# Pooled attention and a gated convolution FFN on one core: the division in two steps on VectorE or ScalarE, the score scale in the keys, the order written out anew

## The chip, the cores and the metric

The kernel runs on one core of one Trainium2 chip. The metric is the device time of one execution in microseconds (us), the median of several runs. Engines are named as in the profile: PE is TensorE's matmul stream and PEld its weight loads, DVE is VectorE, ACT is ScalarE, POOL is GpSimd, SP is SyncE. A "q" behind an engine's name means its queue of DMA issues. L697 is line 697 of the kernel before.

## The reference

The inputs are `q`, `k`, `v` of shape (8, 8, 576, 64) (batch, heads, sequence, head size), and the weights `w_in` (512 x 1024), `conv_w` (3 x 1024) and `w_out` (1024 x 512). The output is (8, 576, 512) in float32.

```python
# attention over keys and values that are averaged in runs of 8
k_p = k.reshape(B, H, 72, 8, D).mean(axis=3)
v_p = v.reshape(B, H, 72, 8, D).mean(axis=3)
scores = matmul(q, k_p.transpose(0, 1, 3, 2)) / sqrt(D)
attn = exp(scores - max(scores, axis=-1))
x = matmul(attn / sum(attn, axis=-1), v_p)        # heads side by side: (8, 576, 512)

# gated FFN with a convolution of three taps over the sequence
h = maximum(x @ w_in, 0)
conv_out[s] = sum over k of conv_w[k] * h[s + k - 1]
out = (h * sigmoid(conv_out)) @ w_out
```

## The kernel before

The eight sequences (`b` = 0 to 7) are worked in four groups of two (`g` = 0 to 3). A group's 1152 rows of queries are cut into tiles of 128 rows (`t` = 0 to 8; group 0 has ten, since it splits the tile that both sequences share). Attention is done tile by tile, the FFN sequence by sequence, so that the attention of a later sequence runs beside the FFN of an earlier one.

A tile of attention takes these steps, each a function:

- `att_scores` (PE): the scores of eight heads against 72 pooled keys each, into two PSUM banks.
- `att_max` (VectorE, L608): the negated maximum of each head.
- `att_shift`: it is added to the scores, on VectorE (L620) for 27 tiles and as a matmul on PE (L628) for group 0.
- `att_exp` (ScalarE, L646): the exponent, with the scale 1/64 (an eighth for the mean over 8 keys, which the pooling leaves as a sum, and an eighth for the head size).
- `att_turn` and `att_copy`, or a transposing DMA (`att_send`, L666, groups 2 and 3): the transposed weights.
- `att_values` (PE, L682): the products with the values; a 65th column of each head holds the sum of the weights.
- `att_divide` (VectorE): a reciprocal of the eight sums (L695), and at once the product with it (L697), which gives the tile `x`.
- `att_turn_out` and `att_copy_out`, or a transposing DMA (`att_out`, L706): `x` transposed, as the FFN's input.

Keys are prepared by a pooling matrix `pm` on PE for sequences 0 and 1, and for the others by three additions on VectorE (`pool_pair`, L439) and a matmul with a selection of the identity (`turn_pair` with `pick`, `turn_keys`). Values are prepared by three additions (`prep_v`, L486) and a product with a mask (L490), all on VectorE. Queries are transposed on PE (`prep_q`), in halves or in quarters of the array, and copied (`copy_q`, L534) by VectorE or ScalarE; those of sequences 6 and 7 by a transposing DMA (`q_send`).

The FFN of a sequence: `ffn_in` (PE, L727) and `ffn_relu` (ScalarE, L736) for eight blocks of 128 features; the convolution either on PE (`ffn_conv`, L889), with `ffn_tanh` (L914) and `ffn_gate` (L925, L927), or by taps, for six half sequences (`TAPS`): the middle tap on ScalarE (L862), the two others on VectorE (`ffn_tap`, L864), then `ffn_tap_tanh` (L869) and `ffn_tap_gate`. The gate's product with `h` is L935 (`ffn_times`) behind PE's convolution and L876 behind the taps; "product" below is one of these 16 instructions. Then `ffn_out` (PE, L943), `ffn_copy` (L954) on either engine, and `ffn_store` (L966).

The order of all this is written out by hand. `add` makes a graph of operations, each with the engines that it may run on and a planner's price in us. `order` reads three tables: `ORDER` names each operation in turn (twice its number, plus 1 for the second of its engines, -1 for a fill, a matmul without use that keeps PE busy), `FORMS` says which form of the array a step takes, `PLACES` which buffer or bank. So the program of each engine's queue is fixed, and each engine works through its own in order; across engines it waits by semaphores only where data or buffers need it. All loads go through POOL's queue but the first three, the transposing DMAs and most stores through SP's.

Buffers come in rings: `"v": 3`, `"qp": 4` (queries as loaded), `"x": 4`. The output tiles of group 3 (`late`) lie in halves of the `qp` buffers.

Of the kernel before, what the change touches and what calls it, by code (L numbers as in the profile page):

```python
# [33 lines left out]
class Graph:  # L34
# [32 lines left out]
    SHIFT_PE = ((0, 0), (0, 1), (0, 2), (0, 3), (0, 4), (0, 5), (0, 6), (0, 7), (0, 8), (0, 9))  # L67
    TURN_DMA = 2
    BANKS = 8
    ORDER = (  # L70
# [52 lines left out]
    )  # L123
    FORMS = (
        1, 0, 1, 0, 1, 1, 1, 0, 0, 0, 0, 1, 1, 0, 0, 1, 1, 0, 0, 0, 0, 1, 1, 0, 0, 0, 0, 1, 0, 0, 0, 1, 1, 1, 1, 0, 1, 1, 1, 1,
    )
    PLACES = (
# [50 lines left out]
def kernel(  # L178
# [23 lines left out]
    KW = 2 * Sp  # L202
    SLOTS = 24
    NJ = 5
    KP = NJ * P

    groups = [[0, 1], [2, 3], [4, 5], [6, 7]]
    where = {b: (g, i) for g, bs in enumerate(groups) for i, b in enumerate(bs)}
# [1210 lines left out]
```

## Time and profile before

| | |
|---|---|
| median of 3 runs | 217.14 us (216.84 to 217.48) |
| span of the profiled execution | 216.5 us |
| between that span and the median of the runs | 0.6 us |
| busy: PE, DVE, ACT | 201.9, 193.2, 162.7 us |
| matmuls and their weight loads | 2753 each |
| instructions on DVE, ACT | 334, 278 |
| mean granted clock of TensorE | 0.992 |

The span runs from the first to the last instruction of the profiled execution; a run's time has a little more around it, taken here as the 0.6 us to the median. The busy time of an engine is the time in which at least one of its instructions runs, so that two which overlap at their ends count once. A row of groups names line, engine, operation, output and inputs, count, then busy us and the mean ns of one, then the idle time in front of them and what ended it. A row of the timeline has start and length in us.

### The profile page before, as it was taken

To read this page: it belongs to the slowest core of one execution; us is meant where nothing else is said; L and a number is where in the kernel's file an instruction comes from. 1 tells how busy PE (TensorE), PEld (TensorE's weight loads), DVE (VectorE), ACT (ScalarE), POOL (GpSimd) and SP (SyncE) were. 2 spreads that over 40 slices of the span, in tenths; PEclk is the share of its full clock that TensorE was granted. 3 is DMA by queue.
4 is the path that set the end of the run, shared out by engine and by line. 5 is a ranking of instruction groups with operands and counts; after the bars stand their busy time and mean duration, and the time that the engine had idled before them with its cause. 6 is when DMAs were issued, how large, how long until landed. Compare 5 with 4: busy or idle time off the path is not lost.

```text
span 216.5 us, 6617 instructions
## 1 busy us (share of the span) xinstructions
PE 201.9 (93%) x2753; PEld 137.0 (63%) x2753; DVE 193.2 (89%) x334; ACT 162.7 (75%) x278; POOL 41.5 (19%) x78
## 2 busy tenths in 40 slices
PE   7599999969999999999999899989999999999992
PEld 3557778855788776766776675665656666654451
DVE  7598989999999999999999799999899999998621
ACT  2548885896998887787497594878979999997420
POOL 8644330050052101000000030002201210370000
PEclk9799999999999999999999999999999999999999
DMA  6999999999999999969687634576347745602685
GB/s 210 227 207 209 206 207 208 210 205 206 207 205 206 154 153 179 158 164 165 131 111 100 136 74 89 58 156 148 78 104 153 158 100 123 145 0 51 169 242 171
DMA packets 48833, 33.46 MB, mean 155 GB/s; under 512 B 28300, under 2 KB 43812, under 8 KB 48804
## 3 DMA queue, kind: packets, MB, share of 16 engines
q0 software_dynamic: 15216, 15.40, 43.5%
q1 hardware_dynamic: 32512, 16.13, 36.6%
q10 hardware_dynamic: 1076, 1.52, 2.5%
q8 instruction: 21, 0.34, 0.7%
q14 instruction: 8, 0.07, 0.1%
HBM read 32.52 MB, written 9.44 MB: 194 GB/s over the span
## 4 chain that ended last, share of the span: by engine, by line
PE 45%; DVE 34%; issue 6%; ACT 6%; DMA 5%; SPq 2%; DVEq 0%
PE psum L943 20%; PE psum L727 16%; DVE negm L608 7%; DVE x L697 6%; DVE sd L620 4%; DVE gT L935 4%; DMA hT<-in_k_dram 3%; DVE v L486 3%; DVE gT L927 3%; PE psum L889 2%; DMA out_dram<-osb 2%; DVE r L695 2%; PE psum L682 2%; ACT e L646 2%; DVE gT L925 1%
## 5 line engine op out<-in xcount | busy, mean ns | idle before, releaser
L727 PE MATMUL psum<-xT,w_in_sb 128*128 128x288 bf16 x512 | 74.1, 286 | 2.2 <-DMA xT<-x 1.1
L943 PE MATMUL psum<-w_out_sb,gT 128*128 128x512 bf16 (+1 forms) x296 | 69.5, 374 | 0.7 <-DVE gT L935 0.6
L727 PEld LDWEIGHTS <-w_in_sb 128*128 128x128 bf16 x512 | 47.9, 98 | 19.1 <-issue 2.0
L736 ACT ACTIVATE hT<-psum 128x576 bf16<-128x576 f32 x64 | 40.3, 650 | 14.0 <-PE psum L727 13.4
L943 PEld LDWEIGHTS <-gT 128*128 128x128 bf16 x296 | 27.3, 98 | 26.5 <-issue 0.9
L864 DVE SCALAR_TENSOR_TENSOR tg<-hT,convw,tg 128x576 f32<-128x576 bf16 x48 | 37.6, 815 | 0.5
L608 DVE TENSOR_REDUCE negm<-psum 128x8 f32<-128x576 f32 (+2 forms) x37 | 27.5, 752 | 2.3 <-PE psum L582 1.6
L697 DVE TENSOR_TENSOR x<-psum,r 128x512 bf16<-128x512 f32 (+1 forms) x37 | 25.6, 691 | 1.4
L811 POOL COPY hT<-hT 128x126 bf16<-128x126 bf16 x16 | 7.5, 467 | 97.6 <-ACT hT L736 80.1
L620 DVE TENSOR_TENSOR sd<-psum,negm 128x576 f32<-128x576 f32 x27 | 20.2, 753 | 0.5
L682 PE MATMUL psum<-vm,eT 128*128 128x130 bf16 (+5 forms) x240 | 18.9, 222 | 1.1 <-DVE x L697 0.7
L646 ACT ACTIVATE e<-sd 128x576 bf16<-128x576 f32 x27 | 18.2, 685 | 1.3 <-DVE sd L620 1.1
L954 ACT COPY osb<-psum 128x512 f32<-128x512 f32 x27 | 15.7, 585 | 4.4 <-PE psum L943 4.2
L889 PE MATMUL psum<-hT,dw 64*64 64x288 bf16 (+2 forms) x608 | 18.7, 261 | 0.1
L682 PEld LDWEIGHTS <-eT 128*128 128x128 bf16 (+1 forms) x240 | 15.3, 100 | 5.4 <-DMA eT<-e 1.2
L862 ACT ACTIVATE tg<-hT,convw 128x576 f32<-128x576 bf16 x24 | 18.1, 772 | 0.1
L889 PEld LDWEIGHTS <-dw 64*64 64x64 bf16 x608 | 14.8, 107 | 4.6 <-issue 3.7
L869 ACT ACTIVATE gT<-tg 128x576 bf16<-128x576 f32 x24 | 16.3, 683 | 0.7 <-DVE tg L864 0.5
L914 ACT ACTIVATE gT<-psum 128x576 bf16<-128x576 f32 x20 | 12.9, 651 | 3.9 <-PE psum L889 2.7
L914 ACT ACTIVATE tg<-psum 128x576 bf16<-128x576 f32 x20 | 13.0, 652 | 2.6 <-PE psum L889 1.4
L935 DVE TENSOR_TENSOR gT<-gT,hT 128x2304 bf16<-128x2304 bf16 x10 | 13.5, 1352 | 0.1
L486 DVE TENSOR_TENSOR v<-v 128x1280 bf16<-128x1280 bf16 (+2 forms) x24 | 13.0, 540 | 0.2
(84 smaller groups left out, 234.2 us busy)
## 6 DMA issues: line engine op xcount, KB each, us to landing
out_dram<-osb SPq DMA_DIRECT2D x54, 128.0 KB, 2.4
v<-in_v_dram POOLq DMA_DIRECT2D x8, 512.0 KB, 13.1
qp<-in_q_dram POOLq DMA_DIRECT2D x7, 576.0 KB, 14.4
kk<-in_k_dram POOLq DMA_DIRECT2D x3, 1152.0 KB, 14.6
out_dram<-qp ACTq DMA_DIRECT2D x10, 128.0 KB, 2.7
hT<-in_k_dram SPq DMA_DIRECT2D x2, 576.0 KB, 5.0
w_in_sb<-in_moe_w_in_dram POOLq DMA_DIRECT2D x2, 512.0 KB, 14.2
w_out_sb<-in_moe_w_out_dram POOLq DMA_DIRECT2D x1, 1024.0 KB, 24.7
```

The lines of the kernel that those rows point to most:

```text
L608: nc.vector.tensor_reduce(out=a["m"][0:rows], in_=a["s"][0:rows, :, 0:2 * KW].rearrange("p a (h s) -> p a h s", s=Sp), axis=AX.X, op=OP.ma ...
L620: nc.vector.tensor_tensor(out=a["d"][0:rows], in0=a["s"][0:rows, :, 0:2 * KW].rearrange("p a (h s) -> p a h s", s=Sp), in1=a["m"][0:rows]. ...
L646: nc.scalar.activation(out=dst, in_=src, func=ACT.Exp, scale=1.0 / (POOL * 8.0),)
L682: nc.tensor.matmul(out=a["o"][lo:hi, h // 4, (h % 4) * (D + 1):(h % 4 + x1 - x0) * (D + 1)], lhsT=a["eT"][:, j, lo:hi], rhs=buf("vm", b)[: ...
L697: nc.vector.tensor_tensor(out=a["x"][0:rows].rearrange("p (a h d) -> p a h d", a=2, d=D), in0=ov[:, :, :, 0:D], in1=r[0:rows].unsqueeze(3) ...
L727: nc.tensor.matmul(out=banks(ps)[:, j, 0:SC], lhsT=w_in_block(dc, fb), rhs=buf("xT", g)[:, dc, i * S + j * SC:i * S + (j + 1) * SC], start ...
L736: nc.scalar.activation(out=h_of(b)[:, fb].rearrange("p (a s) -> p a s", a=2), in_=banks(ps)[:, :, 0:SC], func=ACT.Relu, scale=0.5,)
L864: nc.vector.scalar_tensor_tensor(out=acc, in0=h, scalar=w, in1=acc, op0=OP.mult, op1=OP.add)
L889: nc.tensor.matmul(out=banks(pss[r ^ c])[c * D:(c + 1) * D, j, lo:hi], lhsT=dw[r * D:(r + 1) * D, tap * n_fb + fb, :], rhs=hT[r * D:(r + 1 ...
L914: nc.scalar.activation(out=t.rearrange("p (a s) -> p a s", a=2), in_=banks(ps)[:, :, 0:SC], func=ACT.Tanh, scale=0.5,)
L935: nc.vector.tensor_tensor(out=gate, in0=gate, in1=h_of(b)[:, four], op=OP.mult)
L943: nc.tensor.matmul(out=bank(ps)[0:rows, columns], lhsT=buf("gT", g)[:, fb, t * P:t * P + rows], rhs=w_out_sb[:, fb, columns], start=(fb == 0),
```

## The change

- The division becomes two steps of the graph: `att_invert` (the reciprocal, VectorE) and `att_divide` (the product, VectorE or ScalarE), which `ORDER` may place apart. On ScalarE the product is eight activations, one for each head, with the head's reciprocal as a column of scales.
- The product behind the taps' gate, so far the second instruction of `ffn_tap_gate`, becomes a step of its own, `ffn_times`.
- The scale 1/64 leaves the exponent. It stands in the pooling matrix, and in `ident_k`, an identity times 1/64 from which `pick` and `turn_keys` take their columns.
- `att_exp` can work head by head with the negated maximum as bias; the list of tiles that do so, `EIGHT`, is empty.
- The late output tiles stand behind the query copies and transposes of sequences 4 to 7, where it was those of sequence 7.
- `ORDER`, `FORMS` and `PLACES` are new as a whole: other engines for some copies, other forms for some score and query steps (six score tiles and one query in quarters that were in larger parts), 28 fills where there were 17, another order of the loads and of everything else.

```diff
+    EIGHT = ()
     ORDER = (
...
+    KSCALE = 1.0 / (POOL * 8.0)
+    ident_k = const.tile([P, P], BF16, name="ident_k")
...
     def clear_pool_matrix():
-        nc.vector.memset(pm[0:TB, :, 0:Sp], 1.0)
+        nc.vector.memset(pm[0:TB, :, 0:Sp], KSCALE)
...
     def build_pick():
+        nc.vector.tensor_scalar(out=ident_k, in0=ident, scalar1=KSCALE, scalar2=None, op0=OP.mult)
...
             func=ACT.Exp,
-            scale=1.0 / (POOL * 8.0),
...
-    def att_divide(g, t):
+    def att_heads(g, t):
+        return att[g, t]["o"][0:rows_of(g, t), :, 0:4 * (D + 1)].rearrange("p a (h d) -> p a h d", d=D + 1)
+
+    def att_invert(g, t):
+        nc.vector.reciprocal(out=buf("r", g, t)[0:rows_of(g, t)], in_=att_heads(g, t)[:, :, :, D])
+
+    def att_divide(g, t, engine):
         a, rows = att[g, t], rows_of(g, t)
-        r = buf("r", g, t)
-        nc.vector.reciprocal(out=r[0:rows], in_=ov[:, :, :, D])
+        ov, r = att_heads(g, t), buf("r", g, t)
         a["x"] = buf("x", g, t)
+        if engine == "ACT":
+            for n in range(H):
+                nc.scalar.activation(
+                    out=a["x"][0:rows, n * D:(n + 1) * D],
+                    in_=ov[:, n // 4, n % 4, 0:D],
+                    func=ACT.Identity,
+                    scale=r[0:rows, n // 4, n % 4:n % 4 + 1],
+                )
+            return
         nc.vector.tensor_tensor(
...
     def ffn_tap_gate(b, f4):
         nc.vector.tensor_scalar(out=gate, in0=gate, scalar1=1.0, scalar2=None, op0=OP.add)
-        nc.vector.tensor_tensor(out=gate, in0=gate, in1=h_of(b)[:, four], op=OP.mult)
...
-        o = add(dve(0.2, 0.69), key, lambda: att_divide(g, t), after=[o], uses=[x, rr, big])
+        o = add({"DVE": 0.115}, key, lambda: att_invert(g, t), after=[o], uses=[rr, big])
+        o = add({"DVE": 0.61, "ACT": 0.82}, key, None, after=[o], uses=[x, rr, big])
+        o.emit = lambda o=o: att_divide(g, t, o.engine)
...
-            gated = add(dve(0.78, 1.39), w, lambda f4=f4: ffn_tap_gate(b, f4), after=tanh, uses=[htok[b], gtok[g]])
+            o = add(dve(0.78), w, lambda f4=f4: ffn_tap_gate(b, f4), after=tanh, uses=[gtok[g]])
+            gated = add(dve(1.39), w, lambda f4=f4: ffn_times(b, f4), after=[o], uses=[htok[b], gtok[g]])
...
-            osb, free = (token("late", g, t), qdone[7, 0]) if g == 3 else (token("osb", g, t), [])
+            osb, free = (token("late", g, t), [x for n in range(4, B) for x in qdone[n, 0]]) if g == 3 else (token("osb", g, t), [])
```

More of the change, by code (lines that the diff above doesn't have):

```diff
@@ L70 @@
     ORDER = (
[52 rows of a table removed]
[55 rows of a table added]
     )
     FORMS = (
-        1, 0, 1, 0, 1, 1, 1, 0, 0, 0, 0, 1, 1, 0, 0, 1, 1, 0, 0, 0, 0, 1, 1, 0, 0, 0, 0, 1, 0, 0, 0, 1, 1, 1, 1, 0, 1, 1, 1, 1,
+        1, 1, 0, 0, 1, 1, 1, 1, 1, 1, 1, 1, 1, 1, 1, 0, 1, 1, 1, 1, 1, 0, 1, 0, 0, 0, 0, 1, 1, 0, 0, 1, 1, 1, 1, 1, 1, 1, 1, 1,
     )
     PLACES = (
[17 rows of a table removed]
[18 rows of a table added]
     )
@@ L260, with by_head @@
     add = graph.add
+    def by_head(g, t):
+        return (g, t) in Graph.EIGHT
     def shift_by_dve(g, t):
@@ L375, in build_pick @@
                     out=pick[:, hh].rearrange("p (s f a e) -> p s f a e", s=2, f=2, a=2)[:, :, f],
-                    in_=ident.rearrange("p (s a hh f e) -> p s a hh f e", s=2, a=2, hh=2, f=2)[:, :, :, hh, f],
+                    in_=ident_k.rearrange("p (s a hh f e) -> p s a hh f e", s=2, a=2, hh=2, f=2)[:, :, :, hh, f],
                 )
@@ L470, in turn_keys @@
                     lhsT=buf("kk", g)[:, c, 0:D],
-                    rhs=ident[:, i * D:(i + 1) * D],
+                    rhs=ident_k[:, i * D:(i + 1) * D],
                     start=True,
@@ L640, in att_exp @@
         e = a["e"] = buf("e", g, t)
+        if by_head(g, t):
+            for n in range(H):
+                r, k = n // 4, n % 4
+                at = (k // 2 * 4 + r * 2 + k % 2 if a["by_rows"] else n) * Sp
+                nc.scalar.activation(
+                    out=e[0:rows, at:at + Sp],
+                    in_=a["s"][0:rows, r, k * Sp:(k + 1) * Sp],
+                    func=ACT.Exp,
+                    bias=a["m"][0:rows, r, k:k + 1],
+                )
+            return
         src = a["d"][0:rows].rearrange("p a h s -> p a (h s)") if shift_by_dve(g, t) else a["s"][0:rows, :, 0:2 * KW]
@@ L689, in att_values @@
                 )
-    def att_divide(g, t):
+    def att_heads(g, t):
[3 more added lines that the diff above has]
+    def att_divide(g, t, engine):
         a, rows = att[g, t], rows_of(g, t)
-        ov = a["o"][0:rows, :, 0:4 * (D + 1)].rearrange("p a (h d) -> p a h d", d=D + 1)
-        r = buf("r", g, t)
-        nc.vector.reciprocal(out=r[0:rows], in_=ov[:, :, :, D])
+        ov, r = att_heads(g, t), buf("r", g, t)
         a["x"] = buf("x", g, t)
+        if engine == "ACT":
+            for n in range(H):
+                nc.scalar.activation(
+                    out=a["x"][0:rows, n * D:(n + 1) * D],
+                    in_=ov[:, n // 4, n % 4, 0:D],
+                    func=ACT.Identity,
+                    scale=r[0:rows, n // 4, n % 4:n % 4 + 1],
+                )
+            return
         nc.vector.tensor_tensor(
@@ L872, in ffn_tap_gate @@
         g, i = where[b]
-        four = slice(4 * f4, 4 * f4 + 4)
-        gate = buf("gT", g)[:, four, i * S:(i + 1) * S]
+        gate = buf("gT", g)[:, 4 * f4:4 * f4 + 4, i * S:(i + 1) * S]
         nc.vector.tensor_scalar(out=gate, in0=gate, scalar1=1.0, scalar2=None, op0=OP.add)
-        nc.vector.tensor_tensor(out=gate, in0=gate, in1=h_of(b)[:, four], op=OP.mult)
     def ffn_conv(b, f2, pss):
@@ L1113, in add_pair @@
             t = token("ps", n=2)
-            o = add({"PE": 0.26}, key, lambda b=b, t=t: turn_keys(b, t), after=[prev, c0], uses=[t, kk[g]], mode=HALF, count=36)
+            o = add({"PE": 0.26}, key, lambda b=b, t=t: turn_keys(b, t), after=[prev, picked], uses=[t, kk[g]], mode=HALF, count=36)
             c = add(either(0.76, 0.71), key, None, after=[o], uses=[t, ktok[b]])
@@ L1209, in add_att @@
         o = add(dve(0.75), key, lambda: att_max(g, t), after=[o], uses=[ng, s])
-        if shift_by_dve(g, t):
+        if by_head(g, t):
+            o = add({"ACT": 0.9}, key, lambda: att_exp(g, t), after=[o], uses=[e, s, ng, lim])
+        elif shift_by_dve(g, t):
             sd = token("sd", g, t)
@@ L1326, in add_ffn @@
             if f2 % 2 and cross:
-                gated = add(dve(0.78, 1.39), w + 6 * f2 + Graph.GATE, lambda f4=f4: ffn_tap_gate(b, f4), after=tanh[f4], uses=[htok[b], gtok[g]])
+                o = add(dve(0.78), w + 6 * f2 + Graph.GATE, lambda f4=f4: ffn_tap_gate(b, f4), after=tanh[f4], uses=[gtok[g]])
+                gated = add(dve(1.39), w + 6 * f2 + Graph.GATE, lambda f4=f4: ffn_times(b, f4), after=[o], uses=[htok[b], gtok[g]])
                 gdone.setdefault(b, []).append(gated)
```

142 rows, old and new, of tables (ORDER, PLACES) are left out of this document.

## The prediction

> **What bounds the kernel now.** I read the page first: busy shares, the 40 slices, the chain that ended last.
>
> ```profile
> span 216.5 us, 6617 instructions
> PE 201.9 (93%) x2753; PEld 137.0 (63%) x2753; DVE 193.2 (89%) x334; ACT 162.7 (75%) x278; POOL 41.5 (19%) x78
> DVE  7598989999999999999999799999899999998621
> ACT  2548885896998887787497594878979999997420
> PEclk9799999999999999999999999999999999999999
> PE 45%; DVE 34%; issue 6%; ACT 6%; DMA 5%; SPq 2%; DVEq 0%
> ```
>
> VectorE (DVE) is nearly full from the third slice to the 36th, but the chain belongs to TensorE (PE) for more of the span. Where one hands over to the other stands in the chain in order of time, its last part (start, length, what), and the stretches say how full each engine is (columns: stretch, width, then busy time of PE, PEld, DVE, ACT and POOL, clock, DMA).
>
> ```profile
> 142.52 0.61 DVE x L697
> ...
> 144.72 0.51 PE psum L682 x6
> ...
> 199.10 13.16 PE psum L943 x68
> ...
> 212.28 0.42 DVE qp L954
> ```
>
> ```profile
> 100.00:120.00 20.00, 18.68 (x343) 13.66 (x340) 19.56 (x36) 13.51 (x23) 0.00 (x0) 1.00 0.86 131
> 120.00:140.00 20.00, 19.91 (x256) 13.14 (x257) 18.34 (x30) 14.96 (x26) 3.21 (x8) 1.00 0.48 85
> 140.00:160.00 20.00, 18.91 (x215) 11.64 (x208) 19.15 (x31) 16.68 (x30) 3.37 (x8) 1.00 0.58 124
> 160.00:180.00 20.00, 20.00 (x142) 12.78 (x141) 19.76 (x30) 18.45 (x32) 3.09 (x8) 1.00 0.60 130
> 180.00:190.00 10.00, 10.00 (x67) 6.36 (x65) 9.72 (x13) 9.88 (x18) 2.35 (x4) 1.00 0.57 133
> ```
>
> Until 144.7 VectorE sets the pace: attention and preparation pass through it, and PE waits for their tiles. From 144.72 to 212.28 the chain is PE work back to back, while VectorE stays 96 to 99% busy. So time is won by less VectorE work ahead of the hand-over (PE then starts its full stretch earlier) and about as much less behind it (or VectorE becomes the late one). ScalarE (ACT) has 25 to 32% of room from 100 to 140 and almost none from 160 to 190: 28.3 of 30 us.
>
> **VectorE: the division.** The timeline of VectorE around one division (start, length):
>
> ```profile
> 123.05 0.76 DVE L620 TENSOR_TENSOR sd<-psum,negm 128x576 f32<-128x576 f32 x1
> 123.72 0.20 DVE L695 RECIPROCAL r<-psum 128x8 f32<-128x8 f32 x1
> 123.95 0.69 DVE L697 TENSOR_TENSOR x<-psum,r 128x512 bf16<-128x512 f32 x1
> 124.56 0.45 DVE L925 TENSOR_SCALAR gT<-gT 128x1152 bf16<-128x1152 bf16 x1
> ```
>
> The reciprocal starts 0.09 us before the shift in front of it ends; the multiplication, which needs the reciprocal, waits 0.03 past its end. A division costs 124.56 - 123.72 = 0.84 us, of which the reciprocal holds 0.23. Behind it something that doesn't need it could start after 0.20 - 0.09 = 0.11, so standing apart saves 0.12. Written out, the new order keeps 31 multiplications on VectorE; in only 11 of them another VectorE operation stands between reciprocal and multiplication. Six go to ScalarE: tiles (2,2), (2,0), (2,6), (3,2), (3,1), (3,6), as (group, tile). Before: 37 x 0.84 = 31.1 us. After: 20 x 0.84 + 11 x 0.72 + 6 x 0.11 = 25.4. That is **-5.7**. Other neighbours where one needs the one before change in number from 29 to 28 (shift behind its own maximum 13 to 10, tap behind a tap of its block 7 to 13, product behind its own gate 9 to 5): -0.1.
>
> [...]
>
> **VectorE: copies that change engine.** Groups (busy, mean ns of one):
>
> ```profile
> L458 ACT CAST kT<-psum 64x288 bf16<-64x288 f32 x8 | 3.1, 394 | 0.1
> L534 DVE COPY qT<-psum 128x1152 bf16<-128x1152 bf16 x5 | 3.8, 758 | 1.3 <-PE psum L520 1.3
> L534 DVE COPY qT<-psum 128x512 bf16<-128x512 bf16 x1 | 0.4, 425 | 0.1
> L671 DVE COPY eT<-psum 128x640 bf16<-128x640 bf16 x3 | 1.5, 484 | 0.4 <-ACT kT L431 0.4
> L722 DVE COPY xT<-psum 128x512 bf16<-128x512 bf16 x4 | 1.6, 415 | 0.0
> L954 DVE COPY qp<-psum 128x512 f32<-128x512 f32 x3 | 2.1, 689 | 6.0 <-PE psum L943 6.0
> L294 DVE CAST kk<-hT 128x1152 bf16<-128x1152 f32 x1 | 0.7, 742 | 0.0
> ```
>
> Each less 0.09 of overlap. To VectorE: two pair copies (2 x 0.30 by ScalarE's row, VectorE has none), one 512-wide q copy (0.34), two x copies (0.33 and, half as wide, 0.2), one q cast (0.35, as the q copy), one output copy (0.60), the scaled identity (0.1, estimated from these). From it: one 1152-wide q copy (0.67), one e copy (0.39), the k cast (0.65). Net **+0.8**. Two more output copies move to VectorE, but behind the last product of its program, where it idles for PE: nothing.
>
> Sum up to VectorE's last product: -5.7 - 0.1 + 0.8 = **-5.0**.
>
> **The hand-over.** Take PE's value products of tile (3,4), whose division is the piece at 142.52. In both orders exactly the same PE steps stand in front of them, fills left out (17 before, 28 after, placed where PE would wait). VectorE's work in front of them: 29 divisions, after the change 16 whole, 9 apart, 4 with ScalarE: -4.0; one maximum fewer -0.7; four shifts fewer behind their own maximum -0.5; a tap behind a tap +0.1; copies +0.2. That is -4.9: nearly all of the saving lies ahead of the hand-over, and PE's work behind it is the same. The tail is the same too: VectorE's last product (next fence) ends at 203.16, and PE's products for the last sequence's five output tiles follow it, then a copy and a store; after the change the last product is one with taps instead of one with PE's convolution, with the same five tiles behind it.
>
> ```profile
> 201.80 1.36 DVE L935 TENSOR_TENSOR gT<-gT,hT 128x2304 bf16<-128x2304 bf16 x1
> ```
>
> **ScalarE: eight pieces for one.** No row shows a 64-wide activation; these bound it (timeline, then groups):
>
> ```profile
> 151.30 1.44 ACT L862 ACTIVATE tg<-hT,convw 128x576 f32<-128x576 bf16 x2
> 152.63 0.58 ACT L954 COPY osb<-psum 128x512 f32<-128x512 f32 x1
> 153.62 1.74 ACT L736 ACTIVATE hT<-psum 128x576 bf16<-128x576 f32 x3 [0.40 <-PE psum L727]
> ```
>
> ```profile
> L954 ACT COPY osb<-psum 128x512 f32<-128x512 f32 x27 | 15.7, 585 | 4.4 <-PE psum L943 4.2
> L722 ACT COPY xT<-psum 128x256 bf16<-128x256 bf16 x2 | 0.7, 371 | 0.0
> ```
>
> 585 - 371 over 256 columns is 0.836 ns a column. L862, the only activation with a scale column as the divide has, takes 1.33 / 2 = 0.665 us in a row, less 576 columns 0.184 fixed; 64 columns add 0.053: 0.24 us, eight are **1.9 us**. From below, without a price for the scale column (L736, three in 1.74): 0.58 less 0.48 leaves 0.10 fixed, a piece is 0.15 and eight are 1.2. I take 1.9, since its row has the same operand; the planner's price in the diff is 0.82. Six make 11.4 us more on ScalarE, less what leaves with the copies above (the same list, the other way, and two output copies more). The first four, group 2's three and (3,2), stand ahead of the hand-over, where the stretches from 100 to 140 leave ScalarE 11.5 us idle for their 7.6: hidden. The other two stand behind it, (3,1) and (3,6). The first has 3.3 us of room in its stretch of 20, which covers it; the second falls where 28.3 of 30 are taken, and I put its 1.9 us at 94% on the path: **+1.8**. What queues behind a divide on ScalarE is the next relu, tanh or exponent, and behind those PE's banks.
>
> **Edits at nothing.** The 1/64 goes into the pooling matrix and the identity as a power of two, no instruction but the scaled identity; the exponent's scale was part of its instruction. The per-head exponent has an empty list. The gate split is two instructions as before. The late buffers' wait is for q copies and transposes of sequences 4 to 7, long done at the first store of group 3. Transposes of one q in quarters instead of halves and six score tiles in quarters leave PE's time within a few tenths. SP's queue has the q transpose of sequence 6 in front of the first two e transposes instead of behind them; its load comes long before either is due. At the start PE's fills begin behind three more clears; half clock covers the second slice, where this group runs:
>
> ```profile
> 9.37 1.29 PE L406 MATMUL psum<-gT,kk 128*64 128x144 bf16 x18
> ```
>
> Warm, it and its like behind it would be 0.65 shorter each, colder as much longer: 1.3 either way, taken as 0.
>
> **Sum.** Span 216.5 - 5.0 + 1.8 = 213.3. The median of the runs, 217.14, is 0.6 above the span; so **213.9 us**, its own range 212.2 to 215.5.
>
> **Rivals.** *All of it arrives* (ScalarE's room takes all six): 217.1 - 5.0 = 212.1, with a warm start 210.9. For it: PE and VectorE both gain the same 5 us; against it: ScalarE's slices 31 to 36, all at 9.
>
> *ScalarE takes VectorE's place, slower.* Each divide holds ScalarE's queue 1.9 us, and relu, tanh and exponent queued behind it wait; PE waits for their banks. Priced at what exceeds the 0.82 it was placed by, 6 x 1.1 = 6.6: 217.1 - 5.0 + 6.6 = 218.7. It is slower as soon as more than 0.83 us of each divide gets to the path. [...] In the trace 0.184 of a 0.24 piece is fixed. Against this rival: four of six lie in 25 to 32% of room.
>
> *A load comes late.* v of sequence 4 was issued early, into a buffer long free:
>
> ```profile
> 45.59 0.76 POOL L305 DMA_DIRECT2D v<-in_v_dram  x1
> DMA to landing us min/median/max: 18.2/18.2/18.2
> 58.44 0.65 DVE L490 TENSOR_TENSOR vm<-v,mask_wide 128x960 bf16<-128x960 bf16 x1
> 71.87 0.82 DVE L486 TENSOR_TENSOR v<-v 128x1280 bf16<-128x1280 bf16 x1
> ```
>
> It landed at 63.8 and was used at 71.87. In the new order it stands behind two q loads and in the buffer of sequence 2, whose last reader (58.44) ends at 59.1, some 1.7 sooner after the change: issue at 57.4 at best, use due 2.1 sooner, at 69.8. With the 18.2 us of its row it lands at 75.6 and VectorE stands 5.8 us: 219.7. With a queue emptier than at 45, as I expect, it is in time. Half of that is no change: 216.8.
>
> **Chances.** Forecast 0.40; all arrives 0.20; no net change (half of the load's delay, or orders' small waits) 0.10; ScalarE slower 0.22; load late 0.08. Within 0.3% (0.65 us), about what a measurement can tell, is 216.5 to 217.8. Faster: 0.40 + 0.20 + 0.03 of the middle case = 0.63; same 0.07; slower 0.30. The range goes from 210.9 (all, warm) to 218.7 (ScalarE's price), with about a tenth left out on each side.
>
> **What would show it.** Right: VectorE's last product ends near 200; PE's unbroken stretch starts near 140; a reciprocal with a stranger behind it is followed after 0.11; eight pieces take 1.9 us; ScalarE is busy about 10 us longer. Wrong: ScalarE's divide as releaser of waits for relu, tanh or PE's banks above 2 us in sum; an idle VectorE ahead of the v additions of sequence 4; last product not before 203.

## The result, and the profile after

The changed kernel takes 223.64 us (median of 4 runs, 223.22 to 224.42), the kernel before 217.31 us beside it (216.84 to 218.12): ratio 1.030, 95% interval 1.026 to 1.034, slower. The prediction had 213.9 us, in a range of 210.9 to 218.7. Some executions of a kernel take over 1.5% longer than its fastest (three of 12 in the last experiment, up to 227.33 us where the fastest has 216.31); the times and ratios below leave them out.

The page of the changed kernel (span, busy, VectorE in 40 slices, one DMA queue, the chain's shares):

```profile
span 222.1 us, 6965 instructions
...
PE 199.3 (90%) x2890; PEld 135.8 (61%) x2908; DVE 191.1 (86%) x335; ACT 170.8 (77%) x320; POOL 40.7 (18%) x78
...
DVE  7788767969799989899979999999979999999640
...
q8 instruction: 22, 0.36, 0.7%
...
PE 48%; DVE 17%; DMA 11%; ACT 9%; issue 8%; SPq 3%; POOL 2%; DVEq 0%; ACTq 0%; POOLq 0%
```

VectorE is busy 2.1 us less than before, as wanted, and yet the span is 5.6 us longer: of VectorE's slices 5 to 11 only two still have a nine, where before six had one. PE has 137 matmuls and 155 weight loads more. Stretch by stretch, after and then before (stretch, width, busy PE, PEld, DVE, ACT, POOL):

```profile
20.00:60.00 40.00, 33.64 (x758) 24.61 (x758) 31.43 (x55) 28.73 (x49) 8.66 (x15) 1.00 1.23 204
```

```profile
20.00:60.00 40.00, 37.30 (x676) 28.66 (x674) 38.07 (x68) 32.17 (x56) 8.14 (x12) 1.00 1.23 207
```

Between 20 and 60 us all three engines are less busy than before, VectorE by 6.6 us and PE by 3.7, at full clock and with the same load on the DMA. Something stops PE, and the others run dry behind it. The chain of the changed kernel in order of time names it (start, length, what), and shows a divide on ScalarE and the end of the span as well:

```profile
28.80 1.42 issue
...
43.98 1.54 issue
...
56.53 1.58 issue
...
177.53 1.74 ACT x L724 x8
...
211.91 3.54 DMA out_dram<-osb
215.86 0.60 ACT qp L986
216.50 1.05 PE psum L975 x8
217.64 0.42 DVE qp L986
```

"issue" is time in which an engine waits for nothing that the profile shows. PE's timeline around the three places:

```profile
28.42 0.38 PE L531 MATMUL psum<-ident,qp 64*64 64x64 bf16 x24
30.22 0.29 PE L531 MATMUL psum<-ident,qp 64*64 64x64 bf16 x12 [1.42 <-issue]
...
43.13 0.86 PE L921 MATMUL psum<-hT,dw 64*64 64x288 bf16 x26
45.52 0.32 PE L921 MATMUL psum<-hT,dw 64*64 64x63 bf16 x6 [1.53 <-issue]
...
56.15 0.38 PE L975 MATMUL psum<-w_out_sb,gT 128*128 128x512 bf16 x1 [0.16 <-issue]
58.10 1.45 PE L975 MATMUL psum<-w_out_sb,gT 128*128 128x512 bf16 x6 [1.58 <-issue]
```

Each of these stalls falls inside one step, of which all inputs were there: 24 of 36 transposes run, then nothing for 1.4 us, then the other 12. The reading that the experiments below put to the test is that PE's program comes too late. Queue q8, of the kind "instruction", moves 22 packets, 0.36 MB in all, 16 KB each. Number PE's matmuls, weight loads and the 12 entries of its sequencer in order of start: the three stalls stand at 961, 1473 and 1983, which is 193 + 256 n, two off in the last, and one packet arrives for each such 256. (The 193 is read off the stalls.) Worked out from the trace (times in us; "crossed" is when PE starts the instruction at the boundary in front of the block, "stall" the longest pause within a few numbers of its end):

```
after:  block crossed  packet starts  packet ends  PE passes block's end  whole block  stall
 449-705      19.03        +2.97         22.93           24.30               5.27       1.18
 705-961      24.30        +3.71         28.98           30.22               5.92       1.61
 961-1217     30.22        +3.73         34.92           39.83               9.61        -
1217-1473     39.83        +3.35         44.15           45.52               5.69       1.73
1473-1729     45.52        +3.60         50.02           51.44               5.92       0.46
1729-1985     51.44        +4.31         56.65           58.32               6.88       1.95
before, the only one with a stall ahead of 65 us:
1217-1473     39.42        +3.46         43.85           45.15               5.73       0.51
```

Two of the five stalls of the changed kernel have another explanation as well. At 24.30 and at 51.24 the first matmul behind the pause also waits for a copy on ScalarE, and the profile puts the waits down to that:

```profile
PE psum L593 <- ACT xT L756: 1.1, 1, 1.1
...
PE psum L593 <- ACT kT L469: 0.4, 1, 0.4
```

The other three, 5.3 us in all, have none but the program.

In these rows the packet that by this reading holds the next block starts 3.0 to 4.3 us after PE has crossed into the block before it, takes 0.9 to 1.0, and PE goes on 1.2 to 1.7 us behind its end. Where PE stood, a block of 256 instructions took 5.3 to 6.9 us; the one that the changed kernel entered at 92.54 us, with its packet 1.0 us later, took 4.5 and had no stall. The lag is long while the queue of the loads (q0) fills the DMA (the changed kernel's slices 2 to 11, up to 61 us, all at nine tenths or more, with 187 to 212 GB/s): over both kernels 2.0 to 4.3 us in the 15 blocks crossed up to 60 us, 1.7 to 2.5 in the five later ones beside loads, 0.1 to 0.6 where next to nothing else moves, and anything from 0.2 to 2.6 beside the transfers of queue q1; where PE's instructions are long the packet comes up to 1.5 us ahead of the crossing. Behind 65 us no block is late: PE passes its end 1.8 us or more after the packet.

No packet of the two kernels starts more than one block and 1.5 us ahead of PE, and the stalls of 1.6, 1.7 and 2.0 us in the table are the ones that the profile puts down to nothing else.

The balance, up to VectorE's last product (which ends at 207.62, before at 203.16): VectorE's instructions take 3.7 us less, its idle times of over 0.12 us take 8.2 more, 6.8 of them between 20 and 60 us. Behind the last product 14.5 us follow where it was 13.4. That is +4.5 and +1.1, the 5.6 us of the span.

### The profile page after: what moved, and what is told of

It reads as the page before. It is cut to its first block, busy times and chain, and to the rows that moved or that the text cites. A ratio compares the mean times of both kernels' runs of the same rounds, so it can differ in the third digit from the quotient of the medians.

```text
span 222.1 us, 6965 instructions
## 1 busy us (share of the span) xinstructions
PE 199.3 (90%) x2890; PEld 135.8 (61%) x2908; DVE 191.1 (86%) x335; ACT 170.8 (77%) x320; POOL 40.7 (18%) x78
## 4 chain that ended last, share of the span: by engine, by line
PE 48%; DVE 17%; DMA 11%; ACT 9%; issue 8%; SPq 3%; POOL 2%; DVEq 0%; ACTq 0%; POOLq 0%
PE psum L761 17%; PE psum L975 10%; DVE tg L898 9%; DMA kk<-in_k_dram 5%; PE psum L921 5%; PE psum L703 5%; DMA out_dram<-osb 4%; ACT hT L770 2%; DVE gT L967 2%; SPq L998 2%; PE psum L678 2%; PE psum L531 2%; DMA eT<-e 2%; PE psum L593 2%; PE psum L748 2%
## 5 line engine op out<-in xcount | busy, mean ns | idle before, releaser
L761 PE MATMUL psum<-xT,w_in_sb 128*128 128x288 bf16 x512 | 71.4, 286 | 2.5 <-ACT osb L986 1.0
L975 PE MATMUL psum<-w_out_sb,gT 128*128 128x512 bf16 (+1 forms) x278 | 65.8, 373 | 4.0 <-issue 2.2
L770 ACT ACTIVATE hT<-psum 128x576 bf16<-128x576 f32 x64 | 41.2, 661 | 7.2 <-PE psum L761 6.6
L898 DVE SCALAR_TENSOR_TENSOR tg<-hT,convw,tg 128x576 f32<-128x576 bf16 x48 | 38.2, 817 | 1.2 <-ACT tg L896 0.3
L967 DVE TENSOR_TENSOR gT<-gT,hT 128x2304 bf16<-128x2304 bf16 x16 | 21.7, 1369 | 0.2
L731 DVE TENSOR_TENSOR x<-psum,r 128x512 bf16<-128x512 f32 (+1 forms) x31 | 21.1, 683 | 0.7
L921 PEld LDWEIGHTS <-dw 64*64 64x64 bf16 x608 | 15.3, 107 | 5.3 <-issue 4.0
L986 ACT COPY osb<-psum 128x512 f32<-128x512 f32 x25 | 14.7, 591 | 4.3 <-PE psum L975 2.4
```

The costliest lines, as they stand in the source:

```text
L731: nc.vector.tensor_tensor(out=a["x"][0:rows].rearrange("p (a h d) -> p a h d", a=2, d=D), in0=ov[:, :, :, 0:D], in1=r[0:rows].unsqueeze(3) ...
L761: nc.tensor.matmul(out=banks(ps)[:, j, 0:SC], lhsT=w_in_block(dc, fb), rhs=buf("xT", g)[:, dc, i * S + j * SC:i * S + (j + 1) * SC], start ...
L770: nc.scalar.activation(out=h_of(b)[:, fb].rearrange("p (a s) -> p a s", a=2), in_=banks(ps)[:, :, 0:SC], func=ACT.Relu, scale=0.5,)
L898: nc.vector.scalar_tensor_tensor(out=acc, in0=h, scalar=w, in1=acc, op0=OP.mult, op1=OP.add)
L921: nc.tensor.matmul(out=banks(pss[r ^ c])[c * D:(c + 1) * D, j, lo:hi], lhsT=dw[r * D:(r + 1) * D, tap * n_fb + fb, :], rhs=hT[r * D:(r + 1 ...
L967: nc.vector.tensor_tensor(out=gate, in0=gate, in1=h_of(b)[:, four], op=OP.mult)
```

## The experiments

Three theories stood against each other: F, PE's program is fetched too late; D, the divides hold up ScalarE; T, the tail, where ScalarE's copy stands for a store out of a buffer that is used twice. In `ORDER`, an entry of a step is twice its number, plus 1 for its second engine.

**The forms of before in the changed kernel.**

```diff
 FORMS, by step (1: quarters)
-    scores (0,3) (0,6) (0,7) (0,8) (1,3) (1,7) (2,1) (2,3) (2,7): 1
+    ...: 0
-    query steps 1 (both halves), 3 (one), 4 (one): 1
+    ...: 0
-    scores (0,1) (1,1) (1,2): 0
+    ...: 1
```

> The changed kernel with the forms of the kernel before for each score and query step: 16 steps change, 13 of them from quarters back to halves or whole, about 216 PE instructions fewer up to 60 us (5798 in all become about 5510). Theory F (PE's instructions are fetched in blocks of 256, and while the loads saturate the DMA queues a block cannot be run in less than 5.3 to 6.9 us, so PE stands at block ends): the stalls at 24.3, 30.2, 45.5 and 58.1 us go or shrink by two thirds, VectorE's idle from 20 to 60 us falls from 7.9 to about 3, and the time from 223.6 to 219.5 (218.5 to 221). Theory D (ScalarE's divides) and theory T (tail and other waits of the order): no change, 223.6 within 0.7.

Measured 216.94 us where before has 217.87: ratio 0.996 (0.993 to 1.000). Against the changed kernel that is 0.034 of 217 us, 7.3 us (give or take 1.1): the whole loss, and a time below the expected 218.5 to 221. PE's waits for "issue" between 15 and 62 us, of the changed kernel (all, times, longest):

```profile
PEld L531 <- issue: 2.2, 4, 1.5
...
PEld L921 <- issue: 2.1, 2, 1.7
PEld L593 <- issue: 2.1, 5, 1.1
...
PEld L975 <- issue: 1.9, 1, 1.9
```

and with the forms of before (in the kernel that has other late buffers as well, see "The tail"):

```profile
PEld L657 <- issue: 1.0, 2, 0.6
PEld L474 <- issue: 0.9, 1, 0.9
...
PEld L939 <- issue: 0.7, 2, 0.4
```

The one pause that is left at a block's end is that of 0.96 us at number 1473, and VectorE's idle time from 20 to 60 us is 3.5 us there for 8.0 in the changed kernel. F holds; D and T, which touch nothing of this, expected no change.

**The reverse: the kernel before, all in quarters.**

```diff
 FORMS, by step
-    20 score and query steps: 0
+    ...: 1
```

> The kernel before with all of its 20 score and query steps that are whole or in halves put into quarters, about 430 PE instructions more, 360 of them ahead of 70 us; the order of operations, engines and buffers stays. Theory F: PE stands at the ends of blocks of 256 instructions, issue waits of 1 to 2 us at two to four places ahead of 65 us, and 219.5 to 223. Theories D and T, which have nothing to do with PE's instruction count: 217.3 within 0.7 (the planner prices a query step in quarters 0.11 us less).

Measured 221.58 us, ratio 1.018 (1.013 to 1.024): 4.0 us slower, with nothing of the change in it. PE's timeline at the first block's end that is late:

```profile
21.60 0.41 PE L538 MATMUL psum<-ident,qp 64*64 64x64 bf16 x28 [0.21 <-DVE x L715]
23.97 0.26 PE L538 MATMUL psum<-ident,qp 64*64 64x64 bf16 x8 [1.96 <-issue]
```

It is number 705 of the stream, here with no other wait beside it. The expected two to four places were this one of 2.2 us and one of 0.6 us, at 1985.

The 4.0 us need not all be the program, though. The granted clock, in 40 slices of the span, of this run and then of the next one:

```profile
PEclk9799789997699999999999999999999999999998
```

```profile
PEclk9999589999999999999999999999999999999997
```

Beside the 3.4 us from 8.3 that the kernel before has as well, the clock is here at half for 3.4 us from 25.4 and for 6.8 us from 52.7; in the changed kernel it is full up to 220.5. Five of the six executions have a mean clock of 0.965 to 0.983; the sixth, at 0.996, took 219.9 us, 2.0 more than before. In both runs a half clock begins within 1.5 us of the end of the stall of over 2 us; no run shows whether the stall brought it about.

**Is it the count, or the steps?** The fills are cut into four, so that every later instruction has a higher number.

```diff
 def fill(ps):
-    nc.tensor.matmul(out=bank(ps)[:, 0:448], lhsT=blank[:, 0:P], rhs=blank, start=True, stop=True)
+    for x in range(0, 448, 112):
+        nc.tensor.matmul(out=bank(ps)[:, x:x + 112], lhsT=blank[:, 0:P], rhs=blank[:, x:x + 112], ...)
```

> The changed kernel, each of its 28 fills cut into four matmuls of 112 columns for one of 448, so that PE's time for them is about the same and all instructions behind them stand up to 168 further on in the stream (5798 become 5966). Theory F (blocks of 256 instructions): the stalls fall at the same numbers of the stream, 193 + 256 n, so at other operations, 168 instructions earlier in the program; there are again three to six of them of 0.5 to 2 us, and the time is 222 to 226. The rival (those operations wait for something of their own): the stalls stay at the operations where they were, in the middle of the query step that stood 1.42 us and at the same places near 45 and 57 us, and the time is 223.6 to 224.5.

Measured 223.07 us (2 runs, 222.01 and 224.14), ratio 1.027 (1.020 to 1.033). PE's timeline, with the fills cut and then of the changed kernel:

```profile
20.40 0.47 PE L553 MATMUL psum<-ident,qp 64*64 64x64 bf16 x34
22.97 0.74 PE L553 MATMUL psum<-ident,qp 64*64 64x64 bf16 x38 [2.10 <-issue]
```

```profile
20.95 0.80 PE L531 MATMUL psum<-ident,qp 64*64 64x64 bf16 x72
```

The stall at number 705 now falls in the query step of sequence 1, which the changed kernel ran through at 20.95 without a pause; 961 and 1473 pass without one, and 1729 and 1985 stand 0.74 and 0.64 us, each inside a query step. The steps that stood in the changed kernel don't stand here. The stalls go with the numbers, not with the operations.

**The divides back on VectorE.**

```diff
 ORDER
-    divide of (2,2) (2,0) (2,6) (3,2) (3,1) (3,6): ACT
+    ...: DVE
```

> The changed kernel with its six ScalarE divides back on VectorE, at the same place of the order. Theory D (each divide holds ScalarE 1.74 us and what queues behind it comes late): 3 to 5 us faster, 219 to 220.5. Theory F (fetch stalls ahead of 60 us): VectorE has six multiplications of 0.6 to 0.72 more, 3.6 to 4.3 us, of which four stand ahead of the hand-over; 224 to 227, slower or the same.

Measured 225.92 us, ratio 1.039 (1.034 to 1.044); the pauses at 705, 961, 1473 and 1985 are there again, at 1.1 to 1.7 us. D falls. How much the divides on ScalarE gain stays open: the difference of the ratios is 1.8 us (give or take 1.4), but in its profiled execution VectorE also stands 2.2 us at 102 us, behind PE and a transposing DMA of a tile's weights, which it doesn't in that of the changed kernel.

**The edits alone.** The changed code with the three tables of before, each reciprocal and multiplication side by side.

> The changed code with the order, forms and places of the kernel before: reciprocal and multiplication next to each other as before, all on VectorE, the scale in the keys, one more VectorE instruction for the scaled identity. If all of the loss is in the new order, as theories F, D and T have it: 217.3, within 0.4 of the kernel before. If the edits themselves cost (the scaled identity, or the exponent without its scale): 218 to 219.5.

Measured 217.89 us, ratio 1.001 (0.998 to 1.003). The edits cost nothing that can be measured; the loss is in the order and the forms.

**The tail.** First alone, then with the forms.

```diff
 PLACES, late tiles t = 0..8
-    7, 0, 1, 2, 3, 1, 7, 0, 6
+    7, 0, 1, 2, 7, 5, 4, 3, 6
```

> The changed kernel with other buffers for the output tiles of group 3: only the ninth takes a buffer that was used before, and that one was stored first. In the profile of the changed kernel ScalarE's copy stands 8.0 us for a store that reads the buffer, and the end of the span follows 14.5 us behind the last product, 13.4 before. Theory T (tail): that wait is gone, the tail is 13.3 and the time 222.4 (222.0 to 222.9). If PE's products set the tail alone: 223.6 and 14.5 stay.

> Both repairs together, the forms of the kernel before and the other late buffers, with everything else of the change (order, division in two steps, six divides on ScalarE). Forms alone gave 0.996 of before. Theories F and T add up: 215.9 (215.2 to 216.6) where before is 217.6, ratio 0.992. If the tail's wait costs nothing: 0.996 again.

Measured 223.1 us, ratio 1.027 (1.023 to 1.031), where the changed kernel has 1.030: not told apart. With the forms 217.3 us, ratio 1.000 (0.996 to 1.003), no better than the forms alone and 1.4 us above what was expected. T falls, and ScalarE's timeline in the kernel with both suggests why:

```profile
201.96 5.48 ACTq L1016 DMA_DIRECT2D out_dram<-qp  x6
207.53 1.07 ACT L1004 COPY qp<-psum 128x512 f32<-128x512 f32 x2 [7.05 <-DMA out_dram<-qp]
```

The wait is there still, put down to a store, though that buffer's store was the first of all. The copy starts 0.1 us behind the end of six stores that ScalarE issues itself, which hold its queue for 5.5 us with their own waits; in the changed kernel it came 1.2 us behind the end of its six. What went is that, and PE's 0.87 us ahead of its last eight matmuls. Yet the tail is 14.3 us, and not 13.4: the last copy ends 9.5 us behind the last product, as before, but the issue of the last store ends 1.6 us behind that copy instead of 0.9, and the span 3.2 us later instead of 2.9. No run took stores off these queues.

**What standing apart is worth.** In the kernel with both repairs, all apart divisions put together:

```diff
 ORDER, 11 divisions
-    reciprocal, another VectorE step, multiplication
+    another VectorE step, reciprocal, multiplication
```

> The kernel with both repairs, but each of the 11 reciprocals that stood apart put directly in front of its multiplication, everything else the same. By the prediction's price (0.12 us each) 1.3 us slower than that kernel, 217.2 where it has 215.9. If standing apart saves nothing, as a pipeline that empties after each instruction would have it: the same within 0.5.

Measured 217.8 us, ratio 1.000 (0.997 to 1.003), against 1.000 (0.996 to 1.003). In the profiles VectorE's instructions take 1.1 us more side by side, near the 1.3 of the price; at the end it isn't seen. From the other side, in the order of before, where nothing else moves:

```diff
 ORDER of before, 27 of 37 divisions
-    reciprocal, multiplication, another VectorE step
+    reciprocal, another VectorE step, multiplication
```

> The changed code with the order, forms and places of the kernel before (217.9 with reciprocal and multiplication side by side), and one thing moved: in 27 of the 37 divisions another VectorE operation that is ready stands between reciprocal and multiplication. Prediction's price (0.12 to 0.14 each, nothing else changes): 3.2 to 3.8 us less VectorE, of which 20 divisions lie ahead of the hand-over; 214.9 where before is 217.7 (214.0 to 215.8). Rival: the multiplication comes one operation of 0.4 to 1.4 us later, PE's transposes of x and what hangs on them wait, and the saving is lost: 217.7 or slower.

Measured 221.03 us, ratio 1.017 (1.013 to 1.020): slower by 3.5 us than side by side. Groups of VectorE, side by side and then apart (count, busy, mean ns, idle in front and what ended it):

```profile
L747 DVE TENSOR_TENSOR x<-psum,r 128x512 bf16<-128x512 f32 (+1 forms) x37 | 25.6, 691 | 1.3
L732 DVE RECIPROCAL r<-psum 128x8 f32<-128x8 f32 (+1 forms) x37 | 7.4, 199 | 0.0
```

```profile
L747 DVE TENSOR_TENSOR x<-psum,r 128x512 bf16<-128x512 f32 (+1 forms) x37 | 25.0, 684 | 0.5
L732 DVE RECIPROCAL r<-psum 128x8 f32<-128x8 f32 (+1 forms) x37 | 7.2, 199 | 3.9 <-PE psum L719 2.9 <-ACT hT L786 0.6 <-ACT kT L506 0.2
```

The saving is there: the multiplication's idle time falls by 0.8 us, and with the overlaps VectorE's instructions take 2.5 us less, 2.3 of it in the divisions, 0.09 for each one set apart. But PE now waits for the late multiplication:

```profile
PE psum L622 <- DVE x L747: 1.5, 1, 1.5
PE psum L937 <- DVE x L747: 1.5, 1, 1.5
PE psum L777 <- DVE x L747: 1.3, 3, 0.9
...
PE psum L991 <- DVE x L747: 0.4, 1, 0.4
```

4.7 us in these rows, 1.0 us in the one such row side by side, and VectorE's next reciprocal waits 2.9 us for PE. With six multiplications on ScalarE it gets worse:

```diff
 ORDER, on top of that
-    divide of (1,0) (2,1) (2,2) (2,3) (2,5) (2,6): DVE
+    ...: ACT
```

> The same, with six of the multiplications on ScalarE: tiles (1,0), (2,1), (2,2), (2,3), (2,5), (2,6), all ahead of the hand-over, where ScalarE is idle 1 to 3 us of the 3 to 6 us that follow. VectorE loses another 6 x 0.65 = 3.9 us. If ScalarE's room covers their 1.74 us each: 211.9 (211 to 213). If each costs what exceeds its gain, with relu, tanh and exponent late behind it: 215 to 219.

Measured 225.09 us, ratio 1.033 (1.029 to 1.037), above both expectations. Waits of VectorE and of PE:

```profile
DVE r L732 <- PE psum L719: 7.1, 7, 2.4
...
DVE negm L635 <- ACT xT L772: 3.3, 1, 3.3
```

```profile
PE psum L937 <- ACT hT L786: 1.4, 1, 1.4
PE psum L609 <- ACT x L740: 1.3, 2, 0.6
```

ScalarE's room of 1 to 3 us behind each tile was no room: these rows put the new waits down to x itself and to what stands behind the divide in ScalarE's queue. If only the reciprocals are moved, and no multiplication is put off by more than another reciprocal:

> As the kernel with 27 divisions apart, but only where the multiplication isn't put off by more than a reciprocal: six reciprocals one operation earlier (their value products end in time), three pairs with both reciprocals ahead of both multiplications, so 12 of 37 stand apart; order, forms and places otherwise of the kernel before. If the loss with 27 was the late x (PE waiting for the multiplication), it is gone here and the 0.08 to 0.12 each arrive: 216.6 (216.0 to 217.2) where before is 217.7. If standing apart costs in itself, or moves nothing: 217.7 or more.

Measured 216.91 us where before has 217.16, ratio 0.999 (0.997 to 1.002). The loss is gone, as expected if it was the late x. The gain isn't there: the divisions take 1.2 us less in the profile (0.10 for each of the 12), but all of VectorE's instructions together only 0.3 us less than with every pair side by side (the maxima take 0.7 more), so these runs leave open what such a saving is worth.

**Fewer instructions still**, on top of both repairs:

```diff
 FORMS, by step
-    query steps 2 (both halves), 3 (the other half), scores (0,1) (0,4) (0,9): 1
+    ...: 0
```

> The changed kernel with the forms of the kernel before and other late buffers (0.9996 of before), and six more early steps out of quarters: both query steps of sequence 2, one of sequence 3, the scores of tiles (0,1), (0,4), (0,9); about 150 PE instructions fewer ahead of 60 us. Theory F: what is left of the stalls (0.96 us at 44 us) goes, 216.9 (216.2 to 217.6), ratio 0.996. If the halves' longer steps cost as much: the same, 217.6.

Measured 217.79 us where before has 217.16, ratio 1.001 (0.998 to 1.004): no gain over both repairs, though the longest pause at a block's end falls from 0.96 to 0.4 us. Whether the longer steps cost as much as the pause is open. No version here is clearly ahead of the kernel before; the forms alone, at 0.996 with an interval that ends at 1.000, come nearest.

## Why the prediction was wrong

**Edits at nothing: this step failed.** "Transposes of one q in quarters instead of halves and six score tiles in quarters leave PE's time within a few tenths." Undoing these forms gave back 7.3 us. I had priced the steps by PE's time for them and had not asked what it costs PE to be given more and shorter instructions. Without a row for it the price should have been bounded. There was one: before has an "issue" stall of 0.5 us at number 1473. I also had the count of the forms wrong: six is the net of the score tiles. Step by step nine score tiles and four query steps, of three sequences, went to quarters, and three score tiles came back.

That step explains the loss, but not all of the miss: with it undone the gain is 0.8 us (0 to 1.6), where the forecast had 3.2. The rest lies in VectorE's term and at the hand-over, below.

**VectorE, -5.0: the term came as -3.7.** Summing what each instruction adds to VectorE's time, divisions fell by 4.3 us for the forecast 5.7: the reciprocals, 0.12 us each side by side, are 0.16 on average in the new order. The copies are +1.2 for +0.8. The taps are +1.2, the maxima +0.4, the shifts -0.5 and the gates -1.0, which together are near the -0.1; the rest of the -3.7 is in small differences. That a reciprocal is followed after 0.11 us is borne out: in the changed kernel, where one of VectorE's other steps stands behind it, that one starts after 0.12 us in ten cases of 11 and after 0.19 in one; a tile's own multiplication, 20 times next to it, after 0.23 to 0.24. VectorE's timeline:

```profile
115.02 0.21 DVE L716 RECIPROCAL r<-psum 128x8 f32<-128x8 f32 x1
115.14 0.80 DVE L497 TENSOR_TENSOR v<-v 128x1280 bf16<-128x1280 bf16 x1
```

**The hand-over: only half right.** The prediction took each us of VectorE ahead of it as a us of the end, since VectorE was 96 to 99% busy. Its own rows spoke against that: from 120 to 140 us PE was busy 19.91 of 20 us and VectorE 18.34. With 27 divisions apart VectorE had 2.5 us less to do and the kernel took 3.5 us more. A full engine whose results PE waits for is one part of a loop, and the loop's length counts. After the change PE's unbroken stretch from 140 us isn't there: from 147 us to the last product at 207.62 the chain is mostly VectorE's and ScalarE's. Of the three signs of being wrong only that came: a last product not before 203. No wait of 0.2 us or more is put down to a divide on ScalarE. With both repairs the last product ends at 200.73, near the 200 of the forecast, and the span of that execution is 215.0.

**ScalarE, 1.9 us for eight pieces: 1.74 measured.** The group's mean, 331 ns of one piece, is longer than the step between pieces, 1.74 / 8 = 0.22. The rival that made these divides the bound gave 218.7, but moving them back made the kernel no faster: its time was nearer than the forecast's, its mechanism isn't it.

**The late load** of sequence 4 didn't come to be: VectorE has no long idle time ahead of its additions. **The tail** is 1.1 us longer and not the same as forecast. In the changed kernel its chain runs through the stores: those that SyncE issues, the landing of one, ScalarE's copy behind it, PE, the last copy. Changing the buffers gave back 0.2.

**Still open:** why the kernel with both repairs, with 4 us less of VectorE's work, isn't ahead of the kernel before. Against the changed code in the order of before, VectorE's instructions take 3.9 us less, its idle times of over 0.12 us 2.8 more (3.1 of it between 70 and 110 us) and the tail 0.7 more: that is where it goes. The late x of the runs in the order of before is a cause that would fit; in the new order no run took those waits away. That the loads make the fetch late is read from the blocks with and without loads, and wasn't tried with the loads taken away.

## What to carry to other kernels

Count an engine's instructions as well as its time: in the kernels before and after, while loads filled the DMA, a block of 256 of PE's took 5.3 to 6.9 us where PE stood for it, and stalls that a profile calls "issue", in the middle of a step with all its inputs, are the sign to look for. Shorter instructions that save a little of PE's time are better tried behind the loads, where no block was late in these two kernels, than beside them. And before time saved on a full engine is counted, ask which result comes later for it: with 27 multiplications put off by one operation VectorE's instructions took 2.5 us less, PE waited 4.7 us for them where it had waited 1.0, and the kernel took 3.5 us more.

## What the runs showed of the hardware

PE's program came in packets of 16 KB (22 in the changed kernel, 21 before), one for each 256 instructions, and PE stood at blocks' ends, 0.5 to 2.0 us in the six rows of the table that have a stall, when it got there ahead of them. Counted from PE's entry into the block before, in the kernels before and after, a packet started 1.7 to 4.3 us later beside the loads and 0.1 to 0.6 us later with next to no other transfer; beside the loads it took 0.9 to 1.1 us, and where PE stood it went on 1.2 to 1.7 us behind the packet's end. And DMA issues on ScalarE's queue stood in front of the copy behind them: in the kernel with both repairs six stores, with their own waits, held that queue for 5.5 us, the copy started 0.1 us after the last, and the profile put its wait of 7.05 us down to a store.
